# A recurrence and a two-layer network on one core: a new table of due times for the planner, a model of the load queue in it, and a last output tile in two halves

## The chip, the core and the metric

The kernel runs on one core of a Trainium2 chip. The metric is the device time of one launch in microseconds; lower is better. PE is the engine that multiplies matrices, DVE and ACT work on rows of data in SBUF and PSUM, POOL works on SBUF alone and issues some DMAs, SP issues nearly all loads and most stores.

## What is computed

```python
for t in range(S):                      # B=4, H=8, S=768, D=48
    kt, vt, rt = (k[:, :, t], v[:, :, t], r[:, :, t])
    cur = np.einsum('bhd,bhe->bhde', u[None] * kt, vt)
    y[:, :, t] = np.einsum('bhd,bhde->bhe', rt, state + cur)
    state = w[None, :, :, None] * state + np.einsum('bhd,bhe->bhde', kt, vt)
x = y.transpose(0, 2, 1, 3).reshape(B * S, H * D)      # 3072 tokens x 384
h = x @ w_in                                           # 384 x 2048
return ((h * np.cos(h)) @ w_out).astype(np.float32)    # 2048 x 384
```

`w` lies between 0.85 and 0.95, and `w_in` and `w_out` arrive as 64-bit floats.

## The kernel before

**Tiles.** The tokens are cut into 24 chunks of 128 (chunk i is batch i % 4, place i // 4 of the sequence). The recurrence of a chunk is done in closed form: products of `k` and `r` that carry powers of `w`, a causal mask, and a state that is handed from one chunk of a batch to the next. The result of a chunk is a slot of `xh` and `xl` (the value as the sum of two numbers of reduced precision, which PE multiplies at full rate). The network then takes 8 blocks of three chunks; a step is one block and one of 16 slices of 128 hidden columns: nine matmuls for `h` (L302, function `mm_h`, 128x384 each), a cosine gate on ACT and DVE, and nine matmuls for the output (L309, `mm_o`). There are 128 steps. The weights come in as 32 tiles (16 of `w_in`, 16 of `w_out`): a load into one of three `raw` buffers, integer work on DVE (L654, L666), an addition on POOL (L677), a rounding on ACT (L687, `w_in_hi` or `w_out_hi`) and a difference on DVE (L694).

**A chunk.** The first 12 chunks ("early") load `k`, `r` and `v` from SP (L763 and L755). POOL multiplies `r` by `k` (L864), multiplies `k` by its decay (L874) and the product by `u` (L917). PE transposes `k` and `r` (L833); DVE and ACT copy the transposes out (L892 on DVE for `r`, L912 on ACT for `k`); PE multiplies them (L958); ACT writes the diagonal (L942) from a sum of DVE (L923); DVE masks (L963); PE forms the chunk's result (L978, L989) and the state's increment (L1004); ACT and DVE write `xh` and `xl` (L1179, L1184) and DVE the state (L1026, L1027). The last 12 chunks ("late") use other loads and work in halves of 64 tokens; their decay is on POOL (L852).

**Order.** No engine's order is written out by hand. `Plan` holds one `Op` for each piece of work, with an engine, a due time, a cost, a latency, what it follows and which buffers it needs. `one_pass` is a list scheduler: at each point it takes, for the engine that can start first, the operation with the earliest due time among those that can start. `order` repeats it with due times computed backward from the end of the pass before (`latest`), keeps the due times of the best pass, and plays these. What this emits is each engine's order in the program; on the chip each engine then works through its list in order and waits with semaphores. Due times of the first pass come from tables: `CHUNK_DUE` for the early chunks, a rule for the late ones, and `TILE_SHIFT` added to a rule for the first 12 weight tiles. Where the plan leaves PE idle ahead of the first step, `warm_up` puts small matmuls (L1351) that compute nothing.

**Buffers.** An `h` of a step writes a PSUM bank of three (`B_H`, banks 3 to 5), which the early chunks' products also use (`B_ONE`, banks 3 to 7). SP's loads use eight completion semaphores in turn, so a load waits for the one eight places ahead of it in SP's list.

## Time and profile before

| what | value |
|---|---|
| runs | 514.08, 514.42, 516.64 us; median 514.42 |
| the profiled execution | 514.43 us, of which the span from the first to the last instruction is 512.7 us |
| PE busy | 498.7 us, 97% |
| DVE, ACT, POOL busy | 383.6, 314.0, 177.3 us |
| mean granted clock of PE | 0.995 |
| loads and stores | 61.81 MB, 121 GB/s over the span; 80097 of 116657 packets under 512 B |

A busy PE may be waiting inside its pipeline, and its 97% also holds the small matmuls that compute nothing. So the share says little by itself; the stretches of the span have to be read one by one. A row of a timeline gives start and length in microseconds, engine, line, operation, what is written from what, how many, and in brackets the idle time just ahead with what ended it.

### The profile page before, as it was taken

To read this page: it belongs to the slowest core of one execution; us is meant where nothing else is said; L and a number is where in the kernel's file an instruction comes from. 1 tells how busy PE (TensorE), PEld (TensorE's weight loads), DVE (VectorE), ACT (ScalarE), POOL (GpSimd) and SP (SyncE) were. 2 spreads that over 40 slices of the span, in tenths; PEclk is the share of its full clock that TensorE was granted. 3 is DMA by queue.
4 is the path that set the end of the run, shared out by engine and by line. 5 is a ranking of instruction groups with operands and counts; after the bars stand their busy time and mean duration, and the time that the engine had idled before them with its cause. 6 is when DMAs were issued, how large, how long until landed. Compare 5 with 4: busy or idle time off the path is not lost.

```text
span 512.7 us, 14821 instructions
## 1 busy us (share of the span) xinstructions
PE 498.7 (97%) x5836; PEld 472.2 (92%) x5836; DVE 383.6 (75%) x788; ACT 314.0 (61%) x805; POOL 177.3 (35%) x183
## 2 busy tenths in 40 slices
PE   7999899999999999999999999999999999999994
PEld 5777789999999999999999999999999999999994
DVE  6888778889899996566777786767767777756452
ACT  1887676777776676547375665574663746654442
POOL 5876512246544463214426224133044042200000
PEclk9999899999999999999999999999999999999999
DMA  9978526577855875426484837448364475110001
GB/s 139 157 152 153 135 79 181 161 161 147 163 138 126 188 144 92 90 40 114 115 173 124 181 93 181 100 130 200 90 169 118 120 178 149 35 49 1 1 1 53
DMA packets 116657, 61.81 MB, mean 121 GB/s; under 512 B 80097, under 2 KB 112482, under 8 KB 116578
## 3 DMA queue, kind: packets, MB, share of 16 engines
q1 hardware_dynamic: 111250, 53.50, 43.0%
q0 software_dynamic: 5184, 7.08, 9.9%
q8 instruction: 47, 0.77, 0.7%
q14 instruction: 32, 0.26, 0.2%
q10 hardware_dynamic: 144, 0.20, 0.1%
HBM read 48.96 MB, written 11.80 MB: 118 GB/s over the span
## 4 chain that ended last, share of the span: by engine, by line
PE 88%; ACT 0%; issue 0%
PE psum L309 40%; PE psum L302 40%; PE psum L1123 4%; PE psum L1060 1%; PE psum L1076 1%; PE psum L989 1%; PE psum L958 0%; PE psum L978 0%; PE psum L1004 0%; PE psum L833 0%; ACT f L1320 0%; PE psum L605 0%
## 5 line engine op out<-in xcount | busy, mean ns | idle before, releaser
L309 PE MATMUL psum<-w_out_hi,gh 128*128 128x384 f32 x384 | 131.9, 344 | 0.0
L302 PE MATMUL psum<-xh,w_in_hi 128*128 128x384 f32 x384 | 131.5, 342 | 0.0
L309 PE MATMUL psum<-w_out_hi,gl 128*128 128x384 f32 x384 | 129.7, 338 | 0.0
L302 PE MATMUL psum<-xh,w_in_lo 128*128 128x384 f32 x384 | 129.7, 338 | 0.0
L309 PE MATMUL psum<-w_out_lo,gh 128*128 128x384 f32 x384 | 129.5, 337 | 0.0
L302 PE MATMUL psum<-xl,w_in_hi 128*128 128x384 f32 x384 | 129.4, 337 | 0.0
L314 ACT ACTIVATE qi<-psum 128x384 int32<-128x384 f32 (+1 forms) x132 | 62.9, 479 | 79.6 <-PE psum L302 78.8
L317 DVE SCALAR_TENSOR_TENSOR f<-psum,qi 128x384 f32<-128x384 f32 (+1 forms) x132 | 71.0, 540 | 47.4 <-ACT qi L314 46.6
L1293 DVE TENSOR_TENSOR gl<-f,gh 128x384 fp32r<-128x384 f32 (+1 forms) x132 | 83.9, 639 | 28.9 <-ACT gh L1290 28.0
L1290 ACT CAST gh<-f 128x384 fp32r<-128x384 f32 (+1 forms) x132 | 65.8, 501 | 40.0 <-DVE f L1287 20.0
L320 ACT ACTIVATE f<-f 128x384 f32<-128x384 f32 (+1 forms) x132 | 67.6, 514 | 30.9 <-DVE f L317 30.4
L1287 DVE TENSOR_TENSOR f<-psum,f 128x384 f32<-128x384 f32 (+1 forms) x132 | 70.6, 537 | 12.8 <-ACT f L320 10.9
L309 PEld LDWEIGHTS psum<-w_out_hi,gh 128*128 128x128 f32 x384 | 72.0, 187 | 2.4 <-issue 0.2
L302 PEld LDWEIGHTS psum<-xh,w_in_hi 128*128 128x128 f32 x384 | 72.5, 189 | 1.6 <-ACT T L942 0.2
L302 PEld LDWEIGHTS psum<-xl,w_in_hi 128*128 128x128 f32 x384 | 72.6, 189 | 0.0
L302 PEld LDWEIGHTS psum<-xh,w_in_lo 128*128 128x128 f32 x384 | 72.6, 189 | 0.0
L309 PEld LDWEIGHTS psum<-w_out_hi,gl 128*128 128x128 f32 x384 | 72.0, 188 | 0.0
L309 PEld LDWEIGHTS psum<-w_out_lo,gh 128*128 128x128 f32 x384 | 72.0, 187 | 0.0
L852 POOL TENSOR_TENSOR T<-T,decT_k 112x512 f32<-112x512 f32 x12 | 17.0, 1414 | 126.7 <-DVE T L847 50.8
L1335 POOL DMA_DIRECT2D out_dram<-f x36 | 33.3, 1080 | 41.0 <-ACT f L1320 40.6
L677 POOL TENSOR_TENSOR f<-f,raw 128x384 int32<-128x384 int32 x23 | 26.2, 1138 | 48.0 <-ACT gh L1290 15.7
L942 ACT ACTIVATE T<-ident,a 128x128 f32<-128x128 f32 x96 | 30.2, 391 | 1.2 <-DVE a L923 1.2
(124 smaller groups left out, 610.8 us busy)
## 6 DMA issues: line engine op xcount, KB each, us to landing
raw<-in_moe_w_out_dram SPq DMA_DIRECT2D x23, 384.0 KB, 3.6
out_dram<-f POOLq DMA_DIRECT2D x36, 192.0 KB, 5.0
raw<-in_moe_w_in_dram SPq DMA_DIRECT2D x72, 64.0 KB, 2.4
out_dram<-f SPq DMA_DIRECT2D x23, 192.0 KB, 2.0
r_all<-in_r_dram SPq DMA_DIRECT2D x40, 96.0 KB, 2.3
raw<-in_moe_w_in_dram SPq DMA_DIRECT2D x10, 384.0 KB, 4.0
raw<-in_k_dram SPq DMA_DIRECT2D x39, 96.0 KB, 2.2
v<-in_v_dram SPq DMA_DIRECT2D x18, 192.0 KB, 4.4
```

Source lines behind the costliest of these rows:

```text
L302: nc.tensor.matmul(ph, a, b_, start=(i == 0), stop=(i == len(mm) - 1))
L309: nc.tensor.matmul(acc, a[:, ts], b_, start=(first and i == 0), stop=(last and i == 2))
L314: nc.scalar.activation(qi, ph, AF.Copy, scale=INV_2PI, bias=0.25)
L317: nc.vector.scalar_tensor_tensor(q, ph, INV_2PI, qi, op0=ALU.mult, op1=ALU.subtract)
L320: nc.scalar.activation(q, q, AF.Sin, scale=TWO_PI, bias=0.5 * math.pi)
L677: lambda: nc.gpsimd.tensor_tensor(ai(), ai(), cn(), op=ALU.add),
L942: nc.scalar.activation(A[j]()[:, p, :], ident, AF.Copy, scale=ab()[:, h : h + 1])
L1123: nc.tensor.matmul(xv()[G * g : G * g + G, kk, tokens(n)], lhsT, rhs, start=(kk // 2, g) not in opened, stop=True, skip_group_check=True,)
L1287: nc.vector.tensor_tensor(g()[:, cs], ph()[:, cs], q()[:, cs], op=ALU.mult)
L1290: nc.scalar.copy(gh()[:, cs], g()[:, cs])
L1293: nc.vector.tensor_tensor(gl()[:, cs], g()[:, cs], f32(gh())[:, cs], op=ALU.subtract)
L1335: nc.gpsimd.dma_start(dst, ob(), accum_op=ALU.add)
```

## The change

The planner's tables are new: all 24 chunks get a shift on a rule (`CHUNK_SHIFT`), all 32 weight tiles get one (`TILE_SHIFT`), and there is one pass more. The planner now treats the load queue as a resource: an `Op` with `dma` moves bytes for that long, one transfer after the other, SP may run at most 3 us ahead of it, and the latency of a load follows from it. Loads carry smaller costs on SP. Some other costs are new too (0.59 for 0.55 of the transposes, 0.5 for 0.6 and so on); they change no instruction. `u` is tied behind `w` on SP, and the early loads behind `u`; `u` stood second on SP before as well. `w_out`'s first buffer holds 8 of its 16 slices rather than 10. `R_r` is made after `R_k`, `R_v` and `R_a`; all rings keep their sizes. The last output tile is multiplied, copied out and stored in two halves of 192 columns: DVE and SP take the first, ACT both of the second. Small matmuls may now fill planned gaps up to the first output step rather than up to the first `h`.

```diff
-CHUNK_DUE = (-17.2, -100.0, -17.0, -16.6, -14.0, -12.8, -11.2, -10.1, -1.3, 1.2, 13.7, 37.7)
+CHUNK_SHIFT = (
+    -49.0, -43.2, -29.1, -25.3, -15.4, 1.2, 0.3, 0.4, -2.4, -1.4, 2.5, 2.4, -9.8, -52.4, -17.0, 2.6,
...
-PASSES = 6
+PASSES = 7
+DMA_AHEAD, DMA_FIRST, DMA_LAST, DMA_LAND = 3.0, 1.3, 0.6, 1.95
...
-                        feas.append((max(free[eng], r[0], port if o.port else 0.0), o, r[1]))
+                        t = max(free[eng], r[0], port if o.port else 0.0, moved - DMA_AHEAD if o.dma else 0.0)
+                        feas.append((t, o, r[1]))
...
+            if o.dma:
+                moved = max(moved, t + DMA_FIRST) + o.dma
+                o.lat = max(moved + DMA_LAST - o.end, DMA_LAND)
...
-    F_1 = CUTS[-2]
+    F_1 = NF // 2
...
-            nc.tensor.matmul(acc, a[:, ts], b_, start=(first and i == 0), stop=(last and i == 2))
+            nc.tensor.matmul(acc[:, cs], a[:, ts], b_[:, cs], start=(first and i == 0), stop=(last and i == 2))
...
         o_u = op(
             SP,
             -23.9,
-            1.2,
+            0.5,
...
-            lat=4.6,
+            lat=2.0,
+            dma=0.6,
+            behind=o_w,
...
-            l_k = op(SP, due - 5.2, 1.2, (load if late else load_p)(kb, k), ahead, [kb], lat=2.6, line=ln)
+            l_k = op(SP, due - 5.2, 0.5 if late else 1.15, (load if late else load_p)(kb, k), ahead, [kb], line=ln, dma=1.25, behind=o_u)
...
             if i < EARLY:
-                due = CHUNK_DUE[i]
+                due = -1.5 * (EARLY - i) - 1.0
...
+            due += CHUNK_SHIFT[i]
...
+                last = jc == NJ - 1 and f == f1 - 1
+                ends = [slice(0, DM // 2), slice(DM // 2, DM)] if last else [slice(0, DM)]
+                for e, cs in enumerate(ends):
...
+                    eng = DVE if t % 2 or (last and e == 0) else ACT
...
+                    q = ACT if last and eng == ACT else POOL if f0 and not last else SP
```

The tables act only through the order of the instructions. At three places it looks like this (buffer numbers are kept).

**SP, the loads around the first two tiles of `w_in`** (`raw0` and `raw1`; `k2` with the `r_all` next to it are chunk 8's, `early_k0` with the other `r_all` chunk 9's). Before:

```order
L540 DMA raw0_127<-in_moe_w_in_dram 32x2x256 x4
L540 DMA raw0_127<-in_moe_w_in_dram 64x256 x2
L755 DMA early_v2_94<-in_v_dram 128x8x48
L755 DMA v0_81<-in_v_dram 128x8x48
L763 DMA k2_80<-in_k_dram 128x4x48 x2
L763 DMA r_all_77<-in_r_dram 128x4x48 x2
L763 DMA early_k0_89<-in_k_dram 128x4x48 x2
L763 DMA r_all_77<-in_r_dram 128x4x48 x2
L755 DMA v1_82<-in_v_dram 128x8x48
L540 DMA raw1_128<-in_moe_w_in_dram 32x2x256 x4
L540 DMA raw1_128<-in_moe_w_in_dram 64x256 x2
L763 DMA early_k1_90<-in_k_dram 128x4x48 x2
```

After, the same stretch of SP's list:

```order
L778 DMA early_v2_94<-in_v_dram 128x8x48
L778 DMA v0_80<-in_v_dram 128x8x48
L786 DMA r_all_85<-in_r_dram 128x4x48 x2
L786 DMA k2_79<-in_k_dram 128x4x48 x2
L786 DMA r_all_85<-in_r_dram 128x4x48 x2
L554 DMA raw0_127<-in_moe_w_in_dram 32x2x256 x4
L554 DMA raw0_127<-in_moe_w_in_dram 64x256 x2
L786 DMA early_k0_89<-in_k_dram 128x4x48 x2
L778 DMA v1_81<-in_v_dram 128x8x48
L554 DMA raw1_128<-in_moe_w_in_dram 32x2x256 x4
L554 DMA raw1_128<-in_moe_w_in_dram 64x256 x2
L778 DMA v2_82<-in_v_dram 128x8x48
```

Chunk 8's loads and chunk 9's `r` moved ahead of the first weight tile, and chunk 8's `v` (`v2`) moved ahead of chunk 10's `k` and `r`. Up to the loads of chunk 11 (`early_k2`, `early_r1`) the two lists hold the same loads.

**POOL and ACT, ahead of the second step's `h`.** It needs the second tile of `w_in` (`f4_117` with `raw1`). On POOL the names `early_k1` and `f5` belong to chunk 10, `early_k2` to chunk 11. POOL before:

```order
L864 TENSOR_TENSOR f5_118<-early_r0_95,early_k1_90 128x384
L874 TENSOR_TENSOR early_k1_90<-early_k1_90,dec_k_133 128x2x4x48
L917 TENSOR_TENSOR f5_118<-f5_118,u_b_129 128x384
L864 TENSOR_TENSOR f7_120<-early_r1_96,early_k2_91 128x384
L677 TENSOR_TENSOR f4_117<-f4_117,raw1_128 128x384
L874 TENSOR_TENSOR early_k2_91<-early_k2_91,dec_k_133 128x2x4x48
```

POOL after:

```order
L887 TENSOR_TENSOR f5_118<-early_r0_95,early_k1_90 128x384
L897 TENSOR_TENSOR early_k1_90<-early_k1_90,dec_k_133 128x2x4x48
L940 TENSOR_TENSOR f5_118<-f5_118,u_b_129 128x384
L887 TENSOR_TENSOR f6_119<-early_r1_96,early_k2_91 128x384
L897 TENSOR_TENSOR early_k2_91<-early_k2_91,dec_k_133 128x2x4x48
L699 TENSOR_TENSOR f4_117<-f4_117,raw1_128 128x384
```

ACT before, where the `COPY` from PSUM brings out chunk 10's transposed `k`:

```order
L1179 CAST xh_111<-psum_76 128x384
L912 COPY T4_101<-psum_76 112x512
L687 CAST w_in_hi_66<-f4_117 128x3x128
L942 ACTIVATE T3_100<-ident_64,a1_85 128x128 x4
L942 ACTIVATE T0_97<-ident_64,a0_84 128x128 x4
```

ACT after:

```order
L965 ACTIVATE T6_103<-ident_64,a0_83 128x128 x4
L326 ACTIVATE qi0_122<-psum_76 128x384
L709 CAST w_in_hi_66<-f4_117 128x3x128
L935 COPY T5_102<-psum_76 112x512
L965 ACTIVATE T7_104<-ident_64,a0_83 128x128 x2
```

The weight tile's addition moved behind chunk 11's decay on POOL, and chunk 10's copy moved behind the tile's rounding on ACT. On PE the product of chunk 10 (L958, now L981) stands right ahead of the second step's `h` in both; the transposes of chunk 11 stood ahead of that product before and stand behind the `h` of two steps now, and the first step's `h` moved from ahead of the products of chunks 7 and 8 to ahead of the transposes of chunk 10.

**SP, the last stores.** Before, SP's list ended with the first two tiles of the last block, and ACT issued the third (`f0_113`, 128x384):

```order
L1366 TENSOR_LOAD flag_65
L1366 ISA x2
L1333 DMA out_0_dram<-f5_118 128x384
L1333 DMA out_0_dram<-f6_119 128x384
L1367 COMPARE_AND_BRANCH
```

After, it has the first half of the third too, and ACT issues the second half (`f6_119`, 128x192):

```order
L1405 TENSOR_LOAD flag_65
L1405 ISA x2
L1372 DMA out_0_dram<-f5_118 128x384
L1372 DMA out_0_dram<-f1_114 128x384
L1372 DMA out_0_dram<-f4_117 128x192
L1406 COMPARE_AND_BRANCH
```

One store stands there that stood on ACT's list before.

More of the change, by code (lines that the diff above doesn't have):

```diff
@@ L63, with __init__ @@
 class Op:
-    def __init__(self, eng, due, cost, lat, emit, after, bufs, behind, port):
-        self.eng, self.due, self.cost, self.lat, self.emit = eng, due, cost, lat, emit
+    def __init__(self, eng, due, cost, lat, emit, after, bufs, behind, port, dma):
+        self.eng, self.due, self.cost, self.lat, self.emit = eng, round(due, 3), cost, lat, emit
+        self.dma = dma
         self.after = [o for o in after if o is not None]
@@ L86, in __init__, with op @@
         self.lines = {}
-    def op(self, eng, due, cost, emit, after=(), bufs=(), lat=0.2, line=None, port=False):
-        o = Op(eng, due, cost, lat, emit, after, bufs, self.lines.get(line) if line else None, port)
+    def op(self, eng, due, cost, emit, after=(), bufs=(), lat=0.2, line=None, port=False, dma=0.0, behind=None):
+        o = Op(eng, due, cost, lat, emit, after, bufs, self.lines.get(line) if line else behind, port, dma)
         if line:
@@ L191, in one_pass @@
                 cand.setdefault(o.eng, []).append(o)
-        done, port = [], 0.0
+        done, port, moved = [], 0.0, 0.0
         while len(done) < len(self.ops):
@@ L302, in mm_h, with mm_o @@
             nc.tensor.matmul(ph, a, b_, start=(i == 0), stop=(i == len(mm) - 1))
-    def mm_o(acc, g_hi, g_lo, f, t, first, last):
+    def mm_o(acc, g_hi, g_lo, f, t, first, last, cs=slice(0, DM)):
         ts = slice(t * P, (t + 1) * P)
@@ L564, in check_range @@
             raw, ca, cb = Buf(R_raw), Buf(R_f), Buf(R_f)
-            o0 = op(SP, due - 3.0, 1.6, lambda: load_raw(i, raw), [behind], [raw], lat=3.4)
+            o0 = op(SP, due - 3.0, 0.5, lambda: load_raw(i, raw), [behind], [raw], dma=1.3)
             o1 = op(
@@ L639, in cn @@
                 return raw()[:, :, 0]
-            o0 = op(SP, due - 3.5, 1.6 if part else 3.2, lambda: load_raw(i, raw, True), [behind], [raw], lat=3.4)
+            o0 = op(
+                SP,
+                due - 3.5,
+                0.5 if part else 4.2,
+                lambda: load_raw(i, raw, True),
+                [behind],
+                [raw],
+                dma=1.4 if part else 1.5,
+            )
             o2 = op(
@@ L881, in chunk @@
                     due - 2.5,
-                    0.55,
+                    0.59,
                     tr,
-                    [l_r, l_k if first else o_kd, o_pool, o_pads],
+                    [l_r, l_k if first else o_kd, o_pool, o_pads, o_wT],
                     [*rbs, kb, trp, rT, kT],
@@ L934, in early @@
             def early():
-                A = [Buf(R_T) for _ in range(2)]
+                A = [Buf(R_Tc) for _ in range(2)]
                 Ap = [Buf(B_ONE) for _ in range(2)]
@@ L1165, in in_halves @@
                     due - 0.9,
[L1166 removed]
+                    1.16 if c else 0.95,
                     mm_x,
@@ L1313 @@
                     ob = Buf(R_f)
-                    jc = FIRST[n] + t
                     row = (jc % B) * S + (jc // B) * C
-                    dst = out[row : row + C, :]
-                    def cp(acc=acc[t], ob=ob, t=t):
-                        if t % 2 == 0:
-                            nc.scalar.copy(ob(), acc()[:, 0:DM])
-                        else:
-                            nc.vector.tensor_copy(ob(), acc()[:, 0:DM])
-                    oc = op(ACT if t % 2 == 0 else DVE, s + 2.3, 0.45, cp, [oo], [acc[t], ob])
@@ L1327, with cp @@
-                    last = jc == NJ - 1
-                    def st(ob=ob, dst=dst, f0=f0, last=last):
-                        if last:
-                            nc.scalar.dma_start(dst, ob())
-                        elif f0 == 0:
-                            nc.sync.dma_start(dst, ob())
+                    dst = out[row : row + C, cs]
+                    eng = DVE if t % 2 or (last and e == 0) else ACT
+                    def cp(acc=acc[t], ob=ob, eng=eng, cs=cs):
+                        if eng == ACT:
+                            nc.scalar.copy(ob()[:, cs], acc()[:, cs])
+                        else:
+                            nc.vector.tensor_copy(ob()[:, cs], acc()[:, cs])
@@ L1334, in st @@
+                    oc = op(eng, s + 2.3, 0.45 / len(ends), cp, [oo], [acc[t], ob])
+                    q = ACT if last and eng == ACT else POOL if f0 and not last else SP
+                    def st(ob=ob, dst=dst, q=q, cs=cs):
+                        if q == ACT:
+                            nc.scalar.dma_start(dst, ob()[:, cs])
+                        elif q == SP:
+                            nc.sync.dma_start(dst, ob()[:, cs])
                         else:
                             nc.gpsimd.dma_start(dst, ob(), accum_op=ALU.add)
-                    stored[jc] = op(
-                        ACT if last else SP if f0 == 0 else POOL,
+                    stored[jc, e] = op(
+                        q,
```

67 lines of the change are left out of this document (42 added, 25 removed).

## The prediction

> **What bounds the kernel now.** I read the page's shares and chain first, then PE's busy time by stretches, then the timelines of PE, POOL, ACT, DVE and SP around the one stretch with holes, then the end.
>
> ```profile
> PE 88%; ACT 0%; issue 0%
> 7.49:42.25 34.76, 31.48 (x735) 1.00 1.01 156
> 42.25:57.98 15.73, 12.95 (x285) 0.98 0.86 173
> 57.98:62.54 4.56, 4.56 (x20) 0.70 0.25 76
> 62.54:506.00 443.46, 443.31 (x4775) 1.00 0.49 117
> 506.00:512.70 6.70, 0.00 (x0) 0.89 0.29 99
> ```
>
> The chain that ended last is PE. The rows after it give, for a stretch, its length, PE's busy time, the granted clock, the DMA share and GB/s. From 62.54 on PE has 0.15 us of idle in 443 us. It has the same matmuls to do in any order, so what an order can win or lose lies ahead of 62.54 or in the 6.7 us behind the last matmul, unless a new order opens a hole in the full stretch. Ahead of 62.54 the idle time is 3.3 us from 7.49 to 42.25, 2.8 us to 57.98, and the stretch to 62.54 ran at a clock of 0.70. (The first 7.5 us wait for `w` and the first chunk; the order there hardly changes.)
>
> ```profile
> 42.25 0.44 PE L302 MATMUL psum<-xh,w_in_hi 128*128 128x384 f32 x1
> 53.43 1.16 PE L958 MATMUL psum<-T,T 48*128 48x128 f32 x16
> 56.14 0.44 PE L833 MATMUL psum<-ident,early_k 64*112 64x64 f32 x8 [1.55 <-POOL early_k L874]
> 56.64 1.42 PE L958 MATMUL psum<-T,T 48*128 48x128 f32 x16
> 57.98 0.69 PE L302 MATMUL psum<-xh,w_in_hi 128*128 128x384 f32 x1
> 62.54 0.67 PE L978 MATMUL psum<-T,s 48*32 48x128 f32 x32
> ```
>
> The first `h` stands at 42.25, the second only at 57.98, and from there PE never starves. So the second `h` (step 1) is the point to forecast. Ahead of it stand chunk 10's product (56.64) and, ahead of that, chunk 11's transposes, for which PE waited 1.55 us. These waited for POOL:
>
> ```profile
> 48.63 1.02 POOL L864 TENSOR_TENSOR f<-early_r,early_k 128x384 f32<-128x384 f32 x1 [3.47 <-DMA early_r<-in_r_dram]
> 53.13 1.01 POOL L864 TENSOR_TENSOR f<-early_r,early_k 128x384 f32<-128x384 f32 x1 [0.65 <-DVE a L923]
> 54.10 1.02 POOL L677 TENSOR_TENSOR f<-f,raw 128x384 int32<-128x384 int32 x1
> 55.07 1.01 POOL L874 TENSOR_TENSOR early_k<-early_k,dec_k 128x384 f32<-128x384 f32 x1
> 53.04 0.59 ACT L912 COPY T<-psum 112x512 f32<-112x512 f32 x1 [0.92 <-PE psum L833]
> 55.15 0.51 ACT L687 CAST w_in_hi<-f 128x384 fp32r<-128x384 f32 x1 [1.52 <-POOL f L677]
> 55.69 0.81 DVE L694 TENSOR_TENSOR w_in_lo<-f,w_in_hi 128x384 fp32r<-128x384 f32 x1 [0.23 <-ACT w_in_hi L687]
> 56.42 1.34 DVE L963 COPY_PREDICATED T<-upper,psum 128x512 f32<-128x512 int32 x2
> ```
>
> POOL got chunk 10's loads at 48.63 and chunk 11's at 53.13. The second row is put down to DVE, but the program lets that instruction wait for loads alone, so 53.13 is when chunk 11's loads had landed. Behind it POOL does the weight tile (54.10) and chunk 11's decay (55.07). Why they land then is on SP:
>
> ```profile
> 27.08 4.29 SPq L540 DMA_DIRECT2D raw<-in_moe_w_in_dram  x6
> 32.72 2.33 SPq L763 DMA_DIRECT2D k<-in_k_dram  x2
> 37.34 1.97 SPq L763 DMA_DIRECT2D r_all<-in_r_dram  x2
> 39.91 3.42 SPq L540 DMA_DIRECT2D raw<-in_moe_w_in_dram  x6
> 48.02 1.01 SPq L763 DMA_DIRECT2D early_r<-in_r_dram  x2
> 8.00:12.00 4.00, 1.00 1.48 164
> 28.00:30.00 2.00, 1.00 0.65 122
> 30.00:32.00 2.00, 1.00 0.42 114
> 42.00:44.00 2.00, 1.00 0.46 133
> ```
>
> SP is never idle; chunk 11's `r` is issued at 48.02 to 49.03. With the queue full the loads run at 164 GB/s; while SP issues the six pieces of a weight tile they fall to 118 (mean of the two rows from 28 to 32). A pair of loads takes 1.01 us to issue where nothing stops it; the pairs at 32.72 and 37.34 stood 1.32 and 0.96 us longer.
>
> **The change part by part.**
>
> *Loads.* Before chunk 11's pair SP's list holds the same loads in both programs, so its bytes and issue time stay. Moving eight loads ahead of the first weight tile fills the queue ahead of that hole. In the 4 us from 28 to 32 the queue moved (164 - 118) x 4 = 184 KB less than it can, or 1.1 us. Bounds: nothing gained, if the hole only moves with the tile; at most 3.3 us, if the first tile loses its excess over the second (4.29 - 3.42 = 0.87) and the two pairs theirs (2.28), rounded up. I take 1.1, chunk 11's loads at 52.0. Against it, chunk 8's `v` (192 KB, 1.2 us at 164 GB/s) now goes ahead of chunk 10's loads; POOL waited 3.47 us for these, but chunk 10 is needed on PE only just ahead of step 1, so it is covered unless chunk 11's loads come very early.
>
> *The chain from chunk 11's loads to step 1.* Before: 57.98 - 53.13 = 4.85 us. After, POOL does the product, the decay and only then the tile: 1.01 + 1.01 + 1.02 = 3.04. ACT rounds the tile (0.51) and only then copies chunk 10's `k` (0.59); PE then multiplies chunk 10 (1.16) and starts step 1. The sum is 5.30; where two rows of one engine follow each other they overlap by some 0.05 to 0.1, so 5.2. DVE's branch (difference 0.81, one mask 0.67) is shorter: 3.04 + 0.51 + 0.81 + 0.67 = 5.03. That is 0.35 us longer than before. And chunk 11's transposes, done ahead of step 1 before, come behind it now: from 56.14 to 56.64, 0.5 us more to do. Together 0.85 us lost at the same landing. The first `h` that moved late costs nothing while PE waits for step 1 anyway; its cover is that wait, and if the wait went its nine matmuls (1.56 us at full clock, the row of 96.31 below) would stand on the path just as they did before.
>
> *The clock.* Behind the wait of 1.55 us the 18 matmuls of steps 1 and 2 took 62.54 - 57.98 = 4.56 us.
>
> ```profile
> 57.00:58.00 1.00, 1.00 (x15) 0.65 0.63 219
> 58.00:59.00 1.00, 1.00 (x5) 0.50 0.63 177
> 96.31 1.56 PE psum L302 x9
> 11.57 0.66 PE L501 MATMUL psum<-ident,decT_k 128*128 128x128 f32 x4 [1.79 <-DVE decT_k L485]
> 12.00:13.00 1.00, 1.00 (x12) 1.00 1.45 161
> ```
>
> The third row is from the chain: at full clock nine take 1.56, so the drop cost 4.56 - 3.12 = 1.44 us. A wait of 1.79 us at 11.57 cost no clock. So a drop after a wait of this kind happened once in two; the new order has the first `h`, two products and four small matmuls in the last microseconds ahead of step 1, which makes it less likely, and a wait for the loads still there, which makes it likely. I take half, 0.7 us won; bounds 0 and 1.44. The Trainium skill, TensorE: Matmul & The Clock Gate, section "What's actually happening", says that the clock halves after an idle window of about 3.4 us. The trace shows half clock, as it says, but after a wait of 1.55 us. By that rule no wait here is long enough, and the whole 1.44 would be won; the measurement decides.
>
> *The end.*
>
> ```profile
> 505.64 0.34 PE L309 MATMUL psum<-w_out_lo,gh 128*128 128x384 f32 x1
> 506.02 0.48 ACT L1320 COPY f<-psum 128x384 f32<-128x384 f32 x1 [0.58 <-PE psum L309]
> 506.53 0.38 ACTq L1331 DMA_DIRECT2D out_dram<-f  x1
> 505.46 0.94 SPq L1333 DMA_DIRECT2D out_dram<-f  x2
> out_dram<-f ACTq DMA_DIRECT2D x1, 192.0 KB, 3.4
> out_dram<-f SPq DMA_DIRECT2D x23, 192.0 KB, 2.0
> ```
>
> The last copy shrinks by at most half of 0.48, 0.2 us. SP's half can't be issued before SP is done with its two stores (506.40), and an issue of some 0.4 ends at 506.8, against 506.91 for ACT before: 0.1. The last store took 3.4 us to land, the median of the others 2.0; if the wait for the bytes of 192 KB made the difference, halves win up to 1.4, if the three stores share one queue of bytes, nothing. Three matmuls more on PE cost below 0.2. I take 0.4 won, between -0.1 and 1.4.
>
> *All else* (due times of the late chunks, the smaller first buffer of `w_out`, 8 slices rather than 10) acts beside PE's full stretch. What hides it is POOL's, DVE's and ACT's lead over PE; if that went, each late chunk would stall PE.
>
> Sum against the profiled execution, 514.43 (the median of the runs is 514.42, so the two are the same): -1.1 + 0.85 - 0.7 - 0.4 = -1.35, so 513.1 us.
>
> **Rivals.**
> - *The loads come as early as they can.* All 3.3 us of SP's excess go, the clock stays up: -3.3 + 0.85 - 1.44 - 0.4 = -4.3, 510.1 us. For it: the loads fell below 164 GB/s from 28 on for no other reason than the list. Against it: at 164 GB/s the bytes behind the second tile alone hold the last loads back, and chunk 10 would become the wait.
> - *A jam in ACT's list: slower.* Chunk 10's copy, ready at 53.04 before, stands behind the rounding of a tile that stands behind chunk 11 on POOL. If chunk 11's loads land later than before by the 1.2 us of a `v` (the queue's hole sits at the second tile and the last loads come in a burst), nothing is won on loads, and PE waits long enough for the full drop of the clock, as before: 1.2 + 0.85 - 0.1 = +1.95, 516.4, and 517.6 if the second stretch of the drop also covers the transposes and the next products. It decides at a landing of 53.13 - 0.85 + 0.4 = 52.7: any later and the change loses, with the clock as before.
> - *A hole in the full stretch.* If the late chunks' decays on POOL came late by 0.4 us in each of 12, PE would lose 4.8: 518. Against it: the row from 62.54 to 506 has no room for any such wait before, and POOL is busy 35%.
> - *The order changes and the end does not* (the terms cancel) is part of the likeliest case.
>
> **How the numbers follow.** The likeliest case, step 1 within some 2.5 us of the sum, has 0.57, and its own range is 511.5 to 515.5; early loads 0.24; the jam 0.13; the hole 0.06. A change of 0.5% (2.6 us; below 511.9 or above 517.0) is about what a measurement of this kernel can tell from none. Faster than that: nearly all of the early loads and 0.03 of the likeliest, 0.26. Slower: a half of the jam and the hole, 0.12. Between: 0.62. The range reaches from 510.2, near the early loads, to 516.4, the jam, and leaves out the hole and the outer parts of both, 0.2.
>
> **What the changed profile would show.** Right: PE's second `h` (L314 now) near 57.1, with chunk 11's loads on POOL near 52.0 and the tile's addition two microseconds behind them; ACT's copy of chunk 10 directly behind the rounding of the tile; a clock above 0.70 in the five microseconds from the second `h`; PE full behind it; a last store that lands sooner than 3.4 us. Wrong: chunk 11's product on POOL at 53 or later; any idle time of PE beyond 0.5 us behind step 1; or a first `h` that comes behind 53, which would make the weight tile's own chain the wait.

## The result, and the profile after

The changed kernel takes 521.00 us in the median of 6 runs (520.11 to 522.16), the kernel before 514.61 in 6 runs beside it. The ratio of times is 1.0128, with a 95% interval of 1.0104 to 1.0152: slower by 6.6 us, where 513.1 was forecast and 516.4 was the upper end. The profiled execution took 521.13 us with a span of 519.3, against 514.43 and 512.7 before, so 6.6 us of span are to be found.

PE by stretches, after (length, PE busy, granted clock, DMA share, GB/s):

```profile
7.49:42.25 34.76, 30.01 (x615) 0.95 0.92 154
42.25:61.41 19.16, 17.06 (x392) 1.00 0.68 153
61.41:160.00 98.59, 98.59 (x784) 1.00 0.58 137
160.00:260.00 100.00, 98.87 (x1083) 1.00 0.63 130
260.00:511.82 251.82, 251.58 (x2950) 1.00 0.40 101
511.82:519.30 7.48, 0.00 (x1) 0.70 0.25 87
```

Three marks part the span. The second `h` stands at 61.41, not 57.98. From there to the end of the last matmul (511.82) it takes 450.41 us, where it took 505.98 - 57.98 = 448.00 before, although the drop of the clock (1.44 us) is gone. The end takes 7.48 us, where it took 512.70 - 505.98 = 6.72.

| part | before | after | difference | forecast |
|---|---|---|---|---|
| to the second `h` | 57.98 | 61.41 | +3.43 | about -0.75 (landing -1.1, chain +0.35) |
| clock behind it | 1.44 | 0 | -1.44 | -0.7 |
| second `h` to the last matmul, less the clock | 446.56 | 450.41 | +3.85 | +0.5 (transposes) |
| the end | 6.72 | 7.48 | +0.76 | -0.4 |
| sum | | | +6.60 | -1.35 |

**The start.** PE, POOL, DVE and ACT ahead of the second `h`, from their timelines:

```profile
54.29 0.45 PE L314 MATMUL psum<-xh,w_in_hi 128*128 128x384 f32 x1
55.45 0.45 PE L314 MATMUL psum<-xh,w_in_lo 128*128 128x384 f32 x1 [0.54 <-DVE w_in_lo L716]
60.32 1.16 PE L981 MATMUL psum<-T,T 48*128 48x128 f32 x16 [1.19 <-ACT T L935]
61.41 0.44 PE L314 MATMUL psum<-xh,w_in_hi 128*128 128x384 f32 x1
50.81 1.01 POOL L887 TENSOR_TENSOR f<-early_r,early_k 128x384 f32<-128x384 f32 x1 [2.54 <-DMA early_r<-in_r_dram]
53.98 1.01 POOL L887 TENSOR_TENSOR f<-early_r,early_k 128x384 f32<-128x384 f32 x1
56.85 1.02 POOL L699 TENSOR_TENSOR f<-f,raw 128x384 int32<-128x384 int32 x1 [0.56 <-DVE f L688]
53.92 0.55 DVE L946 TENSOR_REDUCE a<-f 128x8 f32<-128x384 f32 x1 [1.71 <-POOL f L940]
54.39 1.01 DVE L716 TENSOR_TENSOR w_in_lo<-f,w_in_hi 128x384 fp32r<-128x384 f32 x1
55.32 1.38 DVE L688 SCALAR_TENSOR_TENSOR f<-raw,f 128x384 int32<-128x384 int32 x1
58.97 0.68 DVE L915 TENSOR_TENSOR T<-psum,decT_r 112x512 f32<-112x512 f32 x1
59.68 0.59 ACT L935 COPY T<-psum 112x512 f32<-112x512 f32 x1 [1.27 <-DVE T L915]
```

All three signs that the prediction called wrong are here: chunk 11's product is at 53.98, the first `h` comes at 54.29 and waits 0.54 us for its tile's difference, and PE is idle behind step 1. But chunk 11 is not what holds PE. Its product stands directly behind chunk 10's three operations on POOL with no wait. The wait is chunk 10's: its loads let POOL start at 50.81, where it was 48.63, and everything of the second `h` follows from there in line. The sum `a` of chunk 10 (L946) stands on DVE ahead of the first tile's difference (L716) and the second tile's mask (L688), and DVE idles 1.71 us until POOL has made what `a` reads. From `a` on DVE works without a gap up to the copy of chunk 10's transposed `r` (L915, 58.97), for which ACT's copy and then PE wait. SP shows why chunk 10 lands late:

```profile
34.06 4.02 SPq L554 DMA_DIRECT2D raw<-in_moe_w_in_dram  x6
39.31 0.50 SPq L778 DMA_DIRECT2D v<-in_v_dram  x1
39.85 4.19 SPq L554 DMA_DIRECT2D raw<-in_moe_w_in_dram  x6
44.09 0.59 SPq L778 DMA_DIRECT2D v<-in_v_dram  x1
45.94 1.01 SPq L786 DMA_DIRECT2D early_r<-in_r_dram  x2
49.28 1.01 SPq L786 DMA_DIRECT2D early_r<-in_r_dram  x2
```

The row at 44.09 is chunk 8's `v`, ahead of chunk 10's `k` and `r`. Nor did the loads behind it go out sooner: the two tiles took 4.02 and 4.19 us to issue, where they took 4.29 and 3.42 before, and chunk 11's `r` was issued at 49.28 rather than 48.02.

**The stretch from 160 to 260 us.** All engines, before and then after (PE, PEld, DVE, ACT, POOL, clock, DMA share, GB/s):

```profile
160.00:260.00 100.00, 100.00 (x924) 98.02 (x923) 75.45 (x138) 59.27 (x139) 38.75 (x38) 1.00 0.53 108
```

```profile
160.00:260.00 100.00, 98.87 (x1083) 94.03 (x1082) 89.08 (x147) 60.80 (x153) 46.02 (x43) 1.00 0.63 130
```

DVE rises from 75 to 89% on nine more instructions. Part of it is the longer instruction, which the chain of waits names on three of its pieces (start, length, what):

```profile
170.91 2.78 DVE gl L1316
204.60 2.24 DVE f L676
226.34 5.50 DVE gl L1316
```

What POOL does at the last of them (timelines of DVE and POOL):

```profile
226.34 5.49 DVE L1316 TENSOR_TENSOR gl<-f,gh 128x384 fp32r<-128x384 f32 x1
225.40 1.78 POOL L1374 DMA_DIRECT2D out_dram<-f  x2 [0.62 <-POOL T L875]
226.76 1.46 POOL L887 TENSOR_TENSOR f<-f,k 128x384 f32<-128x384 f32 x1
227.74 1.73 POOL L875 TENSOR_TENSOR T<-T,decT_r 112x512 f32<-112x512 f32 x1
228.99 1.45 POOL L897 TENSOR_TENSOR k<-k,dec_k 128x384 f32<-128x384 f32 x1
229.99 1.41 POOL L940 TENSOR_TENSOR f<-f,u_b 128x384 f32<-128x384 f32 x1
230.95 1.28 POOL L1374 DMA_DIRECT2D out_dram<-f  x1
```

`gl` is a subtraction of 384 columns with both inputs in SBUF; its usual length is 0.55 us. Here it starts inside a string of POOL operations (several of them back to back, of a late chunk) and ends at 231.83, 0.43 us behind the last of the string's products. Over the program the group of 132 grew by 7.6 us, while the two DVE groups of the gate that read PSUM did not change (L329, 540 ns each in both; 539 for L1310):

```profile
L1293 DVE TENSOR_TENSOR gl<-f,gh 128x384 fp32r<-128x384 f32 (+1 forms) x132 | 83.9, 639 | 28.9 <-ACT gh L1290 28.0
```

```profile
L1316 DVE TENSOR_TENSOR gl<-f,gh 128x384 fp32r<-128x384 f32 (+1 forms) x132 | 91.5, 700 | 24.9 <-ACT gh L1313 24.5
```

The new due times bring late chunks forward: POOL's product of a late chunk starts at 181.5, 229.6 and 251.5 us before, and at 166.4, 207.1, 226.8 and 245.9 after, in the stretch in which DVE, ACT and POOL also convert the tiles of `w_out`.

**The end**, from the chain of waits of the changed kernel:

```profile
511.86 0.37 DVE f L1362
512.23 0.02 issue
512.25 0.32 ACT f L1360
```

```profile
511.19 1.88 SPq L1372 DMA_DIRECT2D out_dram<-f  x3
512.60 0.38 ACTq L1370 DMA_DIRECT2D out_dram<-f  x1
```

The two half copies run one after the other. DVE's half starts only when all matmuls are done, though its own three of the last step start ahead of the other half's, and ACT's half starts only when DVE's is done. ACT's copy so ends at 512.57, 0.75 us behind the last matmul (511.82); before it ended at 506.50, 0.52 behind it. So the copies are 0.23 of the 0.76 us. The last issue of a store ends at 513.07 (506.91 before), and from there to the end of the span it takes 6.23 us, where it took 5.79: half the bytes in the last stores did not end the program sooner.

### The profile page after: what moved, and what is told of

Same layout as the page of the kernel before. It is cut to its first block, busy times and chain, and to the rows that moved or that the text cites. A ratio compares the mean times of both kernels' runs of the same rounds, so it can differ in the third digit from the quotient of the medians.

```text
span 519.3 us, 14857 instructions
## 1 busy us (share of the span) xinstructions
PE 502.5 (97%) x5853; PEld 472.3 (91%) x5853; DVE 394.2 (76%) x789; ACT 315.5 (61%) x805; POOL 177.2 (34%) x183
## 3 DMA queue, kind: packets, MB, share of 16 engines
HBM read 48.96 MB, written 11.80 MB: 117 GB/s over the span
## 4 chain that ended last, share of the span: by engine, by line
PE 85%; DVE 7%; issue 2%; SPq 2%; ACT 1%; DMA 1%; POOL 1%; POOLq 0%; DVEq 0%; ACTq 0%
PE psum L321 38%; PE psum L314 35%; PE psum L1146 3%; DVE gl L1316 2%; PE psum L981 2%; PE psum L1012 1%; PE psum L1083 1%; PE psum L1390 1%; DMA early_r<-in_r_dram 1%; PE psum L1027 1%; PE psum L1099 1%; DVE pq L477 1%; SPq L554 1%; PE psum L856 1%; DVE f L676 1%
## 5 line engine op out<-in xcount | busy, mean ns | idle before, releaser
L1316 DVE TENSOR_TENSOR gl<-f,gh 128x384 fp32r<-128x384 f32 (+1 forms) x132 | 91.5, 700 | 24.9 <-ACT gh L1313 24.5
L329 DVE SCALAR_TENSOR_TENSOR f<-psum,qi 128x384 f32<-128x384 f32 (+1 forms) x132 | 71.0, 540 | 42.8 <-ACT qi L326 42.3
L1310 DVE TENSOR_TENSOR f<-psum,f 128x384 f32<-128x384 f32 (+1 forms) x132 | 70.9, 539 | 18.8 <-ACT f L332 16.8
L699 POOL TENSOR_TENSOR f<-f,raw 128x384 int32<-128x384 int32 x23 | 29.0, 1263 | 51.7 <-DVE f L688 17.3
```

The lines of the kernel that those rows point to most:

```text
L329: nc.vector.scalar_tensor_tensor(q, ph, INV_2PI, qi, op0=ALU.mult, op1=ALU.subtract)
L699: lambda: nc.gpsimd.tensor_tensor(ai(), ai(), cn(), op=ALU.add),
L1310: nc.vector.tensor_tensor(g()[:, cs], ph()[:, cs], q()[:, cs], op=ALU.mult)
L1316: nc.vector.tensor_tensor(gl()[:, cs], g()[:, cs], f32(gh())[:, cs], op=ALU.subtract)
```

## The experiments

All ratios are of times to the kernel before, run beside it on the same chip; "stretch" is the time from the second `h` to the end of the last matmul in the one profiled execution of each. The stretch of the changed kernel is 450.41.

| kernel | ratio (95%) | chunk 10's product | second `h` | stretch |
|---|---|---|---|---|
| e_tail | 1.0103 (1.0054 to 1.0151) | 50.35 | 60.80 | 450.18 |
| e_start | 1.0182 (1.0142 to 1.0222) | 50.77 | 61.38 | 451.72 |
| e_narrow | 1.0050 (1.0021 to 1.0080) | 52.44 | 63.08 | 447.97 |
| e_turns | 1.0046 (1.0017 to 1.0074) | 49.59 | 60.24 | 447.78 |
| x_base | 1.0049 (1.0026 to 1.0072) | 49.49 | 60.44 | 451.85 |
| x_v | 1.0006 (0.9979 to 1.0033) | 48.58 | 58.42 | 447.15 |
| x_chain | 1.0041 (1.0011 to 1.0071) | 50.95 | 60.28 | 447.25 |
| x_both | 1.0017 (0.9988 to 1.0046) | 49.20 | 58.76 | 447.25 |
| e_late | 1.0037 (1.0009 to 1.0064) | 48.96 | 59.41 | 447.39 |
| x_best | 1.0011 (0.9981 to 1.0041) | 49.63 | 59.18 | 447.38 |
| x_best_t | 1.0016 (0.9984 to 1.0048) | 51.60 | 61.16 | 447.71 |
| x_nov | 1.0054 (1.0031 to 1.0076) | 49.79 | 59.34 | 448.84 |
| x_tile | 1.0025 (0.9996 to 1.0054) | 50.08 | 60.05 | 447.44 |
| b_v (before's order) | 1.0002 (0.9984 to 1.0020) | 49.99 | 58.09 | 446.47 |
| b_tr (before's order) | 0.9963 (0.9935 to 0.9991) | 48.35 | 56.65 | 447.47 |

The stretch of x_base holds a wait for a late load, that of x_nov a drop of the clock behind the second `h`. Single executions of one order scatter by a microsecond or so at the second `h`, so the columns of the traces show where time goes and the ratios what it is worth. Part of the scatter goes with PE's clock, of which each execution has its mean on record: among the executions of one kernel, 0.01 less of mean clock goes with some 3.5 us more time (correlation -0.79 over all kernels here).

### The end: the last tile whole again

```diff
-                ends = [slice(0, DM // 2), slice(DM // 2, DM)] if last else [slice(0, DM)]
+                ends = [slice(0, DM)]
...
-                    eng = DVE if t % 2 or (last and e == 0) else ACT
+                    eng = DVE if t % 2 else ACT
```

> The changed kernel with its last output tile multiplied, copied and stored whole again, by ACT. Theory (the halves run one after the other: ACT's copy waits for DVE's): the end from the last matmul goes from 7.5 us back to 6.7, 520.2 us in all. Rival (the 0.8 us is only the landing of a store, which differs from execution to execution): the same time as the changed kernel, 521.0, and 7.3 us or more behind the last matmul.

In its trace one copy ends the chain, and the span ends 517.2 - 510.98 = 6.22 us behind the last matmul:

```profile
511.02 0.48 ACT L1360 COPY f<-psum 128x384 f32<-128x384 f32 x1 [0.58 <-PE psum L321]
```

The five executions profiled with halves took 6.98 (e_turns), 7.48 (the changed kernel), 7.55 (e_narrow), 7.70 (e_late) and 8.0 (e_start), 7.5 on the mean. The twelve with a whole tile took 6.22 to 7.18 (b_tr), 6.7 on the mean. So the halves cost some 0.8 us in the traces, though the two groups overlap. In times it is not separated: 1.0103 against 1.0128, and 1.0049 (x_base, whole) against 1.0046 (e_turns, halves), well inside the intervals.

### The start: two POOL operations moved out of the way of the tables

At 11.83 us DVE's table `decT_k` took 1.50 us rather than 0.68, beside a POOL product (L940 at 11.79). This kernel moves two POOL operations of chunk 2, the product that stood ahead of that one and the chunk's decay, behind chunk 0's decay, to see whether this early collision sets the second `h`.

```diff
+MOVED, MOVED_BEHIND = (61, 62), 21
...
+        moved = sorted((o for o in order[:at] if o.seq in behind), key=lambda o: behind[o.seq])
+        order = [o for o in order[: at + 1] if o.seq not in behind] + moved + order[at + 1 :]
```

> The changed kernel with chunk 2's product and decay moved on POOL behind chunk 0's decay, so that nothing of POOL runs while DVE forms the decay tables. Theory A (POOL held DVE there, and the delay reaches the first steps by way of buffers that come free late and loads that go out late): the tables' copy on ACT starts near 12.6 instead of 14.5 us, PE's second h near 59.3 instead of 61.4, the time 518.8 us. Rival B (the loads set the second h whatever the start does): the copy comes earlier, the second h stays within 0.5 us of 61.4, and the time is 521.0 us.

`decT_k` was 0.69 us again, but four POOL operations now stood back to back beside the seven multiplications of the powers of `w`, which took 4.36 us in place of 3.70. The copy of the decay was at 13.12 in place of 14.54, and the second `h` did not follow: 61.38. Over the traces it does not follow in either direction (copy at 11.12, second `h` at 60.80; 12.41, 60.24). The collision is real, but the tables don't set the second `h`. The time was 523.96 us, where neither theory expected more than 521.0. Why this kernel is slower still (a stretch of 451.72, an end of 8.0) isn't explained by the edit, and stays open.

### The long `gl`: fewer columns on POOL, or POOL taking turns

Two kernels leave the order alone and break only the meeting of DVE with the string on POOL. In the first, the five POOL operations of each late chunk do few columns, and leave the rest of these products out:

```diff
-                    return lambda: nc.gpsimd.tensor_tensor(dst()[0:KP], dst()[0:KP], dec[0:KP], op=ALU.mult)
+                    return lambda: nc.gpsimd.tensor_tensor(dst()[0:KP, 0:1, 0:8], dst()[0:KP, 0:1, 0:8], dec[0:KP, 0:1, 0:8], op=ALU.mult)
...
-                n2.tensor_tensor(in_turn(kb), in_turn(kb), split(dec_k), op=ALU.mult)
+                if late:
+                    n2.tensor_tensor(kb()[:, :, 0:1], kb()[:, :, 0:1], dec_k[:, :, 0:1], op=ALU.mult)
```

> The changed kernel with POOL's five operations of each late chunk done on a few columns only (the rest of these products is left out). Theory C (strings of POOL operations hold DVE's operations that work in SBUF alone, above all gl, and PE waits for these between 160 and 260 us): no gl above 1.5 us there, DVE's busy time in these 100 us falls from 89 to about 78 us, and the time to about 518.0 us. Rival D (the planner put too much DVE work into that stretch, POOL or not): PE still loses 2 us or more between 140 and 260 us, and the time stays at 520.3 or more.

In the second they do all their work, but POOL copies one element of the last `gl` emitted ahead of each, so that it waits until DVE has that `gl` done:

```diff
+    def take_turn():
+        if gl_last[0] is not None:
+            nc.gpsimd.tensor_copy(turn_tok, gl_last[0])
...
+                    if late:
+                        take_turn()
```

> The changed kernel with a read of one element of the gl planned last ahead of each POOL operation of a late chunk, so that POOL waits there for DVE as the plan has it. Theory C: a gl waits for at most one POOL operation, the longest is below 2.5 us instead of 5.5, PE loses under 1 us between 140 and 260 us instead of 3.2, and the time is near 518.6 us. Rival E (the chunks' POOL work comes late by these waits and PE waits for the chunks instead): 521.0 us or more.

e_turns, all engines in the same 100 us, and DVE and POOL at the place of the 5.49 us:

```profile
160.00:260.00 100.00, 100.00 (x1098) 96.98 (x1098) 78.94 (x147) 62.20 (x155) 46.16 (x62) 1.00 0.62 130
```

```profile
223.26 0.56 DVE L1333 TENSOR_TENSOR gl<-f,gh 128x384 fp32r<-128x384 f32 x1
223.96 0.18 POOL L290 COPY turn_tok<-gl 1x1 f32<-1x1 f32 x1
224.10 1.00 POOL L903 TENSOR_TENSOR f<-f,k 128x384 f32<-128x384 f32 x1
```

POOL has as much to do as in the changed kernel (46.16 against 46.02) and DVE the same 147 instructions, but DVE's busy time falls by 10 us and PE has no idle time. The longest `gl` from 140 to 260 us takes 1.36 us. The two kernels give PE the same products in the same order, so their traces can be laid side by side: counted from the second `h`, the changed kernel falls behind e_turns by 0.39 us at 175.2, 0.96 at 209.1, 0.28 at 212.6, 0.44 at 233.5 and 0.27 at 239.8, and by 2.6 over the whole stretch. The first, second and fourth are the next `h` behind the three long pieces of the chain, at 170.91, 204.60 and 226.34. PE had other work beside most of the longest, so 5.49 us on DVE cost it well under 1. Both kernels win about 0.8% (1.0050 and 1.0046 against 1.0128), though one takes POOL's work away and the other only its place in time. So the cause is shown: not how much DVE or POOL has to do, but that they meet.

### The late chunks' due times

The same loss should also go if the two chunks that were pulled forward are left where the rule puts them.

```diff
-            due += CHUNK_SHIFT[i]
+            due += 0.0 if i in (12, 13) else CHUNK_SHIFT[i]
```

> The changed kernel with the shifts of two late chunks alone (12 and 13, which were -9.8 and -52.4 steps) set to zero; the plan up to 120 us and the last 200 us stay. Theory I (these two shifts pulled chunk 13's POOL and DVE work and its loads into the stretch in which the weights are still converted): three late chunks instead of four run ahead of 245 us, DVE is busy about 77 us of the 100 from 160 to 260 us instead of 89, PE loses under 0.7 us from 140 to 260, and the time is 3 to 3.8 us below the changed kernel: 1.0055 of the kernel before. Rival (strings of POOL operations hold DVE wherever the chunk stands): PE still loses 2 us or more, 1.010 or more of the kernel before.

```profile
160.00:260.00 100.00, 100.00 (x981) 97.71 (x980) 71.37 (x141) 59.80 (x144) 39.42 (x38) 1.00 0.54 115
```

DVE is at 71% here, below the 75% before; PE is full, the stretch takes 447.39 and the ratio is 1.0037. So the shifts of chunks 12 and 13 in the table put the strings where they hurt.

### What is left at the start: `v`, and the sum of chunk 10

x_base is the changed kernel with turns and with the last tile whole. From it one operation each is moved, and both, by a loop behind the planner:

```diff
         order = plan.order(PASSES)
+        for moved, behind in MOVES:
+            o = next(o for o in order if o.seq == moved)
+            order.remove(o)
+            order.insert(1 + next(n for n, x in enumerate(order) if x.seq == behind), o)
```

x_v moves chunk 8's `v` behind chunk 10's `r` on SP; x_chain moves the sum `a` of chunk 10 behind the second tile's mask (L688) on DVE; x_both does both.

> The changed kernel with POOL waiting for gl ahead of each late chunk's operations, and with the last tile whole: the base of the next three. Theory: the stretch from the second h to the last matmul as short as before (448 us), the end 6.2 to 6.9 us behind the last matmul; what is left against the kernel before is the second h, at 60.2 to 61.4 us against 58.0, less the drop of the clock that it had: +1 to +2 us, 0.2 to 0.4% slower. Rival (the waits are worth more than PE lost): as fast as before.

> The base, with the load of chunk 8's v moved on SP from ahead of chunk 10's k and r to behind them, as it was before the change. Theory F (the second h stands 10.6 us behind chunk 10's product on POOL, and the bytes ahead of its loads set that): the product of chunk 10 and the second h come 1.2 us earlier, and the time falls by 1.2 us against the base. Rival G (chunk 8's result comes late instead, or the second h waits for chunk 11 or the weight tile): the product comes earlier, the second h by less than 0.4 us.

> The base, with one DVE operation moved: chunk 10's sum (which waits for POOL's three operations on that chunk) from ahead of the first tile's difference to behind the second tile's integer work. Theory H (these two stood in DVE's list behind the wait for chunk 10 though they were ready, and with them the first h, chunk 10's transposes and copies): both run near 51 us, the first h no longer waits for w_in_lo, the second h stands 8.6 us instead of 10.6 behind chunk 10's product, the time falls by 2.0 us against the base. Rival (POOL's and ACT's lists hold the second tile all the same): less than 0.5 us.

> The base with both moves. Theories F and H together: the second h near 57.5 us, the time 3 us below the base and 1 to 2 us below the kernel before. Rival (the second h then waits for chunk 11's loads or for the second tile, at 58.5 or later): 2 us below the base, level with the kernel before.

With `v` moved, the ratio falls by 0.43% (1.0049 to 1.0006) and, with `a` moved as well, by 0.24% (1.0041 to 1.0017). With `a` moved, the distance from chunk 10's product to the second `h` falls from 10.4 to 11.0 us in most executions (9.84 in x_v) to 9.33 and 9.56, so about 1 us in the traces, where 2.0 was expected; the times don't show it (1.0049 to 1.0041, 1.0006 to 1.0017). x_base's own profile shows another price of the early late chunks, a load that DVE waited for, then PE:

```profile
203.72 1.11 DVE L885 STREAM_TRANSPOSE T<-raw 128x512 f32<-128x512 f32 x1 [3.01 <-DMA raw<-in_r_dram]
209.83 0.69 PE L320 MATMUL psum<-xh,w_in_hi 128*128 128x384 f32 x1 [2.73 <-DVE f L1327]
```

That is chunk 13's `r`, and PE ran at a lower clock behind it (0.69 from 210 to 215 us). None of the three other profiles of this set shows it; e_narrow's does (DVE waited 2.57 us at 205.95).

### All repairs together, and each part against them

x_best is the changed kernel with e_late's line, the last tile whole, and both moves. x_best_t adds the turns, x_nov leaves `v` ahead of chunk 10 as the change has it, and x_tile puts the first weight tile's load back ahead of chunk 8's loads.

> All undone that cost: shifts of chunks 12 and 13 zero, the last tile whole, chunk 8's v behind chunk 10's loads, chunk 10's sum behind the second tile's integer work. From the parts: second h near 58.7 us, the stretch from it to the last matmul 447 us, 6.5 us behind it: a span of 512.2, a time of 513.9, 0.999 of the kernel before, against 1.013 of the change. Rival (late loads or held DVE operations still cost in some executions): 1.003 of the kernel before.

> The same with POOL waiting for gl ahead of each late chunk's operations. Theory: with chunk 13 out of the stretch there is nothing left for the waits to save, the same time within 0.5 us. Rival (held gl's still cost PE in some executions): 1 us or more below the last, and less spread.

> The kernel with all undone that cost, but chunk 8's v left ahead of chunk 10's loads, where the change has it. Theory F (the 192 KB ahead of chunk 10's loads make them late): chunk 10's product on POOL 1.2 us later than in the same kernel with the v moved (49.6), second h 1.2 us later, 1.003 of the kernel before. Rival (the landing of chunk 10 scatters by more than the v makes): the product within 0.7 us of 49.6.

> The kernel with all undone that cost, with the first weight tile's load back ahead of the eight loads, where it was before the change: SP's list up to chunk 11's loads is then that of the kernel before. Theory J (loads put ahead of the tile do not gain; the queue holds the same bytes, and the hole only moves): chunk 10's product within 0.7 us of 49.6, the time within 1 us of that kernel, 1.001. Theory K (the tile's place makes chunk 10 late): the product near 48.5 as in the kernel before, second h near 58, 0.998 of the kernel before.

x_best stands at 1.0011 (0.9981 to 1.0041), no different from the kernel before: what was found accounts for the whole loss, within the measurement. The turns add nothing once the chunks are back in place. x_nov, x_tile and b_v ran on another chip than x_best, so they are compared through the kernel before. `v` ahead costs 0.43% once more (1.0054 against 1.0011); the two intervals overlap by a tenth of a per cent, and it is the three pairs together that carry it. The traces of this third pair don't show the path: x_nov has chunk 10's product at 49.79, 0.16 us behind x_best, as its rival had it, and its clock dropped behind the second `h`. In the other two pairs the product came 0.91 and 1.75 us later with `v` ahead. In all three the mean clock with `v` ahead is lower as well, by 0.0014 to 0.0024, which at 3.5 us for 0.01 would be 0.5 to 0.8 of the loss. The place of the first tile's load shows neither gain nor loss (1.0025 against 1.0011).

### Two parts of the change alone, in the kernel before

b_v moves chunk 8's `v` ahead of chunk 10's loads in the order of before. b_tr moves only chunk 11's transposes on PE behind the second step's `h`.

> The kernel before, with chunk 8's v moved ahead of chunk 10's loads on SP, where the change has it, and nothing else. Theory F: chunk 10's product at 49.8 instead of 48.6, still ahead of chunk 11's, so that the second h moves by less than 0.5 us and the time stays, 1.000. Rival (chunk 10's chain is the long one here too): second h at 59.2, 1.002.

> The kernel before with one PE operation moved: chunk 11's transposes from ahead of the second h to behind it, where the change has them. Theory (the transposes waited 1.55 us for POOL and that wait cost the clock 1.44 us): the second h at 57.1 to 57.8 us instead of 58.0 (it then waits for DVE's masks), no drop of the clock behind it, the time 1.0 to 2.0 us below the kernel before. Rival (PE waits as long for the masks, and the clock drops all the same): within 0.5 us of the kernel before.

b_v, PE ahead of the second `h`, and its stretch from 56 to 62 us:

```profile
56.55 0.44 PE L834 MATMUL psum<-ident,early_k 64*112 64x64 f32 x8 [1.55 <-POOL early_k L875]
58.09 0.44 PE L303 MATMUL psum<-xh,w_in_hi 128*128 128x384 f32 x1
56.00:62.00 6.00, 5.45 (x82) 4.89 (x82) 6.00 (x11) 6.00 (x19) 1.46 (x2) 1.00 0.45 133
```

Chunk 10's product on POOL comes 1.36 us later than before (49.99), and nothing follows: the second `h` is at 58.09 (57.98) and the time is the same (1.0002). PE still waits 1.55 us for chunk 11, which covers chunk 10. The same wait as before also left the clock at 1.00. b_tr:

```profile
48.35 1.02 POOL L865 TENSOR_TENSOR f<-early_r,early_k 128x384 f32<-128x384 f32 x1 [2.38 <-DMA early_r<-in_r_dram]
55.10 1.62 PE L959 MATMUL psum<-T,T 48*128 48x128 f32 x16 [0.44 <-DVE T L893]
56.65 0.45 PE L303 MATMUL psum<-xh,w_in_hi 128*128 128x384 f32 x1
58.42 0.44 PE L834 MATMUL psum<-ident,early_k 64*112 64x64 f32 x8
```

The wait for chunk 11 falls to 0.44 us for chunk 10, the second `h` comes at 56.65, and the transposes stand in the full stretch. 513.36 us, 0.9963 (0.9935 to 0.9991): this one move is the part of the change that wins, and it beats both kernels. Its twelve executions have a mean clock of 0.9934, the 35 of the kernel before beside them 0.9900: at 3.5 us for 0.01 that is an estimated 1.2 of the 1.5 us between the means, so most of what the move wins goes with the clock, as its theory had it.

## Why the prediction was wrong, step by step

**Loads, -1.1 forecast.** Wrong, and not by its size alone. Chunk 11's product came at 53.98, 0.85 later, where 52.0 was forecast, and on SP its `r` was issued 1.26 us later than before. The lower bound of that term, "nothing gained, if the hole only moves with the tile", is what x_tile bears out: with the tile ahead again nothing changes. And the step "chunk 10 is needed on PE only just ahead of step 1, so it is covered" failed. Its cover was PE's wait for chunk 11's transposes, and the same change takes them out of the way. With that cover (b_v) a later chunk 10 costs nothing; without it `v` costs 0.43, 0.24 and 0.43% in the three pairs, 1.9 us on the mean, by a later chunk 10 in the traces of two of them. The forecast priced both edits, but each against the order of before. It asked what hides chunk 10 and not what still hides it after the next paragraph's edit.

**The chain, +0.85 forecast.** It was worked out from chunk 11's loads, and the path starts at chunk 10's. From chunk 10's product to the second `h` it is 61.41 - 50.81 = 10.60 against 9.35, +1.25, and the 0.5 us of the transposes stand behind the second `h`, as the forecast had it. Seen whole, the second `h` came 3.43 us later: 2.18 by the product and 1.25 by the distance. Of the 1.25 the place of `a` on DVE is about 1 in the traces; its worth in time wasn't shown. DVE's branch was costed by the lengths of its own instructions, and the wait in front of it, for `a`, was not looked for in the order.

**The clock, -0.7 forecast.** Here 1.44 was gained, the upper bound, in the profiled execution: 1.00 in the row from 42.25 to 61.41 and behind it. That was the luck of one execution. The mean clock over the span is 0.990 on the mean of the six runs of the changed kernel, and 0.989 to 0.991 in the four sets of runs of the kernel before that stand beside the experiments, so the runs show no gain. And in the changed kernel's own profile the clock dropped earlier, behind a stretch in which PE had almost nothing to do:

```profile
10.00:14.00 4.00, 0.62 (x3) 0.89 1.43 180
14.00:18.00 4.00, 4.00 (x45) 0.69 1.45 188
```

What that early drop cost wasn't tried. Also, b_v keeps the wait of 1.55 us and the full clock, and other executions of the changed order dropped (0.71 from 56 to 60 us in e_turns, just ahead of its second `h`). So the drop comes in one execution and not in the next, and the half that was taken was the right kind of number. The Trainium skill, TensorE: Matmul & The Clock Gate, section "What's actually happening", says the window that is watched runs free and the point of change varies from run to run; b_v and the kernel before agree, the same wait with and without a drop. The length of about 3.4 us that it gives for the idle window does not agree: a drop came here behind 1.55 us.

**The end, -0.4 forecast.** +0.76 in the profile. The step "the last copy shrinks by at most half of 0.48" left out that two engines copy out of one PSUM tile: the copies were made one after the other and the first of them behind the last matmul. That is 0.23 of the 0.76; the rest stands behind the copies, where halves were to land sooner and did not, and why stays open. The lower bound, -0.1 for the gain, took SP's queue into account and not this wait. The Trainium skill, PSUM — Partial Sum Buffer, section "PSUM bank collisions raise a hardware error", says that no two of PE, ACT and DVE may touch one bank in the same partitions at the same time, reads against reads included, and that a scheduler puts a dependency between them. The chain of the changed kernel agrees: matmuls to 511.82, DVE's half from 511.86 to 512.23, ACT's from 512.25. By that rule halves in one bank can't overlap, so splitting costs a second copy and a hand-over; the trace can't tell whether the program waits by bank or by tile. What halves in two banks would take wasn't tried.

**All else, 0 forecast, "beside PE's full stretch".** +3.85 where +0.5 stood in the sum, and by the ratios the largest single loss. The 0.5 of the transposes was the chain's; the kernels without long `gl` and without a drop of the clock take 447.2 to 448.0, so the rest, about 2.4 to 3.3, is the meeting of DVE with POOL, and the ratio confirms it (e_turns and e_late 0.8 and 0.9% below the changed kernel). The cover named was "POOL's, DVE's and ACT's lead over PE", and only the sum of it was read: POOL at 35% of the span. DVE's share in the stretch from 160 to 260 us was not read. It was 75% there before, and its longest `gl` was already 2.2 us. The rival "a hole in the full stretch" had the place right, with 518 and a chance of 0.06, and half of the mechanism: it let POOL come late for PE, where POOL came early and held DVE. Its argument against itself, that no such wait stands in the row of before, says nothing of an order that brings four strings into the stretch in place of three. Windows of 100 us for all engines and the longest row of each DVE group would have raised that chance.

**Signs.** The forecast's list of what would show it wrong was good: every entry came true, and the first one (chunk 11 at 53 or later) led to chunk 10 within a few rows.

What stays open: x_best still starts its second `h` at 59.18 where b_tr has 56.65, 0.48% apart in time. In the traces 1.3 of it is the landing of chunk 10 (49.63 against 48.35) and 1.25 the distance from there (9.55 against 8.30). Which of the other moves in the planner's new order makes these two was not tried.

## What to carry to other kernels

When several edits are priced, price each against the order with all others made: name the wait that covers a cost, and look whether another edit of the same change removes that wait. A stretch in which the bound engine is full is not safe for free: read the other engines there by stretches, take the longest instance of each group and not its mean, and see what the neighbour does at that moment. And where two engines share the last piece of work, check in the program's waits that they can run at the same time before counting half.

## What the runs showed of the hardware

- A DVE operation whose inputs both lie in SBUF waits for a whole string of POOL operations: 5.49 us for `gl` in place of 0.55, from within two stores to 0.43 us behind four products, beside another store; 3.63 at 170.05. The DVE groups with an operand in PSUM were not stretched (540 and 539 ns). A conversion of one SBUF input (L676) was held too, 2.24 us on the chain at 204.60. The Trainium skill, SBUF — State Buffer, section "SBUF: two separate sides", says that DVE and GpSimd (POOL here) lock a shared pair of ports for a whole instruction, the loser fully blocked, and names a DVE operation with two SBUF inputs against one of GpSimd that reads SBUF. The trace agrees on who is held; one instruction of POOL is at most 1.8 us in those rows, though, and `gl` was held over all of them, so the wait is for the string.
- A one-element copy on POOL that waits for `gl` costs 0.18 us and moved the string out of the way: DVE's busy time from 160 to 260 us fell from 89.08 to 78.94.
- A planner that has the port as a resource (`port`) does not prevent this. In the plan the held `gl` stands ahead of POOL's operations, but on the chip nothing made POOL wait, and it ran early.
- The clock's drop behind a wait of 1.55 us came in one of two executions with the same wait, at 1.44 us. Over executions of one kernel, time goes with the mean granted clock: some 3.5 us for 0.01.
